# A seven-product scheme for part of the first MoE product, output sums kept in DRAM, and the MoE order set by a list scheduler

## Chip, core and metric

The kernel runs on one core of a Trainium2 chip. The metric is the device time of one execution in microseconds (us); lower is better.

## What is computed

Softcapped attention over 4 batches of 12 heads, 448 tokens of 64 values each, then a dense layer with a SiLU gate. The weights `w_in` (768 x 2048) and `w_out` (2048 x 768) come in as float64, everything else as float32.

```python
scores = scale * np.matmul(q, k.transpose(0, 1, 3, 2))
scores = cap * np.tanh(scores / cap)
scores = scores - np.max(scores, axis=-1, keepdims=True)
attn = np.exp(scores)
attn = attn / (np.sum(attn, axis=-1, keepdims=True) + 1e-09)
x = np.matmul(attn, v)            # then (4, 12, 448, 64) -> (1792, 768)
h = x @ w_in
g = h * (1.0 / (1.0 + np.exp(-h)))
out = g @ w_out
```

## The kernel before

The program has two stages. **Attention** runs first; it writes its result, transposed, into two SBUF tensors: `XH` holds x rounded to float32r and `XL` the remainder. Both are 128 partitions by 6 `d_model` tiles by 1792 tokens. **The MoE stage** follows. Every product there is made of three matmuls, high x high, high x low and low x high, so that float32r matmuls give float32 accuracy.

The 16 `d_ff` tiles of 128 are taken in 8 pairs (`G = 2`). For a tile `f` and a block of tokens `h_unit` (L640) adds up 6 `d_model` tiles x 3 = 18 matmuls in one PSUM bank. Blocks are 512, 512, 512 and 256 tokens. `gate` makes g from it: sigmoid on ACT (L655), product with h on DVE (L656), the rounded `gh` on ACT (L662), the remainder `gl` on DVE (L666). For a pair and 128 tokens `o_unit` (L691) multiplies g by `w_out`: 2 tiles x 3 products x 2 halves of 384 columns = 12 matmuls into two PSUM banks of the pool `ps_s`. `add` (L713, L715) adds the two banks on DVE to an accumulator in SBUF; 14 of these (`acc`) hold the whole output until the last pair, when each is written out from the SP queue (L719).

Weights arrive as float64 by one DMA per tile (`load_w`, L602 and L604) in one of three `RAW` buffers. `decode` turns them into float32 by integer operations (`f64_bits`: L169 on ACT or L167 on DVE, then L171, L172, L176, L180 on DVE, with the scratch tile `KRV`), and splits them into a high part (L623, ACT) and a low part (L625, DVE).

The order of the MoE work is written out by hand in `moe()`: a list of units of PE work, with one small piece of decoding (`bg`) beside each, and `BACK` for the first 19 places. After each unit's matmuls are recorded come, on ACT and DVE, what was put off from the unit before (`LATE`), the piece of decoding, and the unit's own gate or add. In the attention stage `FIRST` says in which slot which decode steps of the first four weight tiles stand. POOL issues DMAs in the attention stage only; among them `fold` (L389), which adds P to T in SBUF as an accumulating DMA.

Of the kernel before, what the change touches and what calls it, by code (L numbers as in the profile page):

```python
# [11 lines left out]
U32 = mybir.dt.uint32  # L12
# [173 lines left out]
def tile_softcap_attention_swish_moe(  # L186
# [41 lines left out]
    KRV = const.tile([128, DM], F32, name="KRV")  # L228
# [3 lines left out]
    psa = ExitStack()  # L232
    pool = lambda st, name, bufs, **kw: st.enter_context(tc.tile_pool(name=name, bufs=bufs, reuse_waits="tile", **kw))
# [14 lines left out]

    ones = a1.tile([128, 3, 32], F32, name="ones")
# [183 lines left out]
    def norm(s, parts=(0, 1, 2)):  # L433
        b, u = s // NU, s % NU
        cs = slice(b * S, (b + 1) * S)
        x = U[s]
        xh, xl = XH[:, 2 * u:2 * u + 2, cs], XL[:, 2 * u:2 * u + 2, cs]
        if 0 in parts:
            nc.vector.tensor_tensor(flat(x), flat(x), flat(RB.pop(s)), ALU.mult)
        if 1 in parts:  # L440
            nc.vector.tensor_copy(xh, x)
        if 2 in parts:
            nc.vector.tensor_tensor(xl, x, xh.bitcast(F32), ALU.subtract)
            if s == NS - 1:
                tail.close()
                MPOOL["acc2"] = pool(core, "acc2", 1, side="right")


    BACK = {
        0: [[], [("d", 3, 3), ("d", 3, 4)]],  # L450
        1: [[("d", 3, 5)], []],
        3: [[("x", NS - 2, 0)], []],
        5: [[], [("x", NS - 1, 0)]],
        6: [[], [("d", 4, 0), ("d", 4, 1)]],
        7: [[], [("d", 4, 2)]],
        8: [[], [("d", 4, 3), ("d", 5, 0), ("d", 5, 1)]],
        10: [[("d", 5, 2)], []],
        11: [[("d", 5, 3)], []],
        12: [[], [("d", 5, 4)]],
        13: [[], [("d", 6, 0), ("d", 6, 1)]],  # L460
        14: [[("d", 6, 2)], [("d", 6, 3)]],
        15: [[("d", 5, 5), ("d", 4, 4)], [("d", 4, 5)]],
        16: [[], [("d", 6, 4)]],
        17: [[("d", 6, 5)], [("d", 7, 0), ("d", 7, 1)]],
        18: [[], [("d", 7, 2), ("d", 7, 3)]],
    }
# [12 lines left out]
        (8, "D1"): (2, (4, 5)),  # L479
        (9, "D1"): (3, (0,)),  # L480
        (10, "D1"): (3, (1,)),
        (11, "D1"): (3, (2,)),
# [59 lines left out]
    def attention():  # L542
# [34 lines left out]
        MPOOL["h"] = pool(psa, "ps_h", 2, space=PSUM)  # L577
        MPOOL["w"] = pool(core, "w", 1)
        MPOOL["g"] = pool(core, "g", 4)
        MPOOL["acc"] = pool(core, "acc", 1)  # L580
        gate(*HEAD[0], (0, 1, 2))
        norm(NS - 3)
# [6 lines left out]
    NTT = NT // 128  # L589
# [3 lines left out]
    blocks = [(t0, min(512, NT - t0)) for t0 in range(0, NT, 512)]  # L593
    NB = len(blocks)

    def load_w(m, eng=nc.sync):
        f, o = divmod(m, 2) if m >= 4 else (m % 2, m // 2)
# [3 lines left out]

# [5 lines left out]
    def decode(m, steps):  # L607

        for step in steps:
            raw = WR[m]  # L610
            if WIDE:
                f64_bits(nc, raw.bitcast(U32).rearrange("p (n t) -> p n t", t=2), KRV, RAW[m % NBUF][:, 0:DM], step, m < 4)
            f = RAW[m % NBUF][:, 0:DM]
            if step == 4:
                if m % 6 < 3:
                    t = W02[m % 6]
                else:
                    t = MPOOL["w"].tile([128, 2 * DM], F32R, tag=f"w{m % 6}", name="w")
                WS[m] = t.rearrange("p (a n) -> p a n", a=2)
                if m < 4:  # L620
                    nc.vector.tensor_copy(WS[m][:, 0], f)
                else:
                    nc.scalar.activation(out=WS[m][:, 0], in_=f, func=AF.Copy)  # L623
            elif step == 5:
                nc.vector.tensor_tensor(WS[m][:, 1], f, WS[m][:, 0].bitcast(F32), ALU.subtract)  # L625
                if m + 3 < 2 * NF:
                    load_w(m + 3, nc.gpsimd if m < 3 else nc.sync)

    GT = {}
    LATE = []  # L630
    HEAD = []

    def h_unit(f, blk, ps=None, kks=range(KDM)):
        t0, n = blocks[blk]
        w = WS[f if f < 2 else 2 * f]
        if ps is None:
            ps = MPOOL["h"].tile([128, 512], F32, tag="h", name="h")
        for kk in kks:
            for a, x in ((0, XH), (0, XL), (1, XH)):
                nc.tensor.matmul(  # L640
                    ps[:, 0:n],
                    w[:, a, kk * 128:(kk + 1) * 128],
                    x[:, kk, t0:t0 + n],
                    start=(kk == 0 and a == 0 and x is XH),
                    stop=(kk == KDM - 1 and a == 1),
                )
        return ps

    GF = {}

    def gate(f, blk, ps, steps=(0, 1)):
        n = blocks[blk][1]
        if 0 in steps:
            gf = MPOOL["g"].tile([128, 512], F32, tag="g", name="gf", bufs=2)
            nc.scalar.activation(out=gf[:, 0:n], in_=ps[:, 0:n], func=AF.Sigmoid)  # L655
            nc.vector.tensor_tensor(gf[:, 0:n], ps[:, 0:n], gf[:, 0:n], ALU.mult)  # L656
            GF[f, blk] = gf
        gf = GF[f, blk]
        if 1 in steps:
            gl = MPOOL["g"].tile([128, 512], F32R, tag="gl", name="gl")  # L660
            gh = MPOOL["g"].tile([128, 512], F32R, tag="gh", name="gh")
            nc.scalar.activation(out=gh[:, 0:n], in_=gf[:, 0:n], func=AF.Copy)  # L662
            GT[f, blk] = (gh, gl)
        if 2 in steps:
            gh, gl = GT[f, blk]
            nc.vector.tensor_tensor(gl[:, 0:n], gf[:, 0:n], gh[:, 0:n].bitcast(F32), ALU.subtract)  # L666
        elif steps == (0, 1):
            LATE.append((f, blk, ps, (2,)))

    def back(slot, n):  # L670
        for kind, j, z in BACK.get(slot, ((), ()))[n]:
            if kind == "d":
                decode(j, (z,))
            elif kind == "x":
                norm(j)

    def o_unit(fp, blk, t):
        ts = slice(t * 128, t * 128 + 128)
        pa = ps_s.tile([128, 2, 512], F32, tag="s", name="s")
        pa = [pa[:, e] for e in range(2)]  # L680
        if (fp, blk, t) == LAST:
            pa[1] = MPOOL["h"].tile([128, 512], F32, tag="h", name="h")

        ends = ((0,), (1,)) if (fp, blk, t) == LAST else ((0, 1),)
        for es in ends:
            for z, f in enumerate(range(G * fp, G * fp + G)):
                g = GT[f, blk]
                w = WS[f + 2 if f < 2 else 2 * f + 1]
                for a, b in ((0, 0), (0, 1), (1, 0)):
                    for e in es:  # L690
                        nc.tensor.matmul(  # L691
                            pa[e][:, 0:NO2],
# [5 lines left out]
        return pa  # L698

    ACC = {}  # L700
    LAST = (NFP - 1, NB - 1, (NT - blocks[-1][0]) // 128 - 1)

    def add(fp, blk, t, pa):
        tt = blocks[blk][0] // 128 + t
        if tt not in ACC:
            ACC[tt] = MPOOL["acc" if tt < 6 else "acc2"].tile([128, DM], F32, name=f"acc{tt}")
        a = ACC[tt]
        last = (fp, blk, t) == LAST
        for e in range(2):
# [137 lines left out]
```

## Time and profile before

| | |
|---|---|
| median of 3 runs | 623.57 us (623.45 to 624.31) |
| the profiled execution | 622.44 us |
| its span, first to last instruction | 620.6 us |
| busy share of the span: PE / DVE / ACT / POOL | 99% / 68% / 42% / 9% |
| granted TensorE clock, mean | 0.999 |
| HBM read / written | 42.47 MB / 5.51 MB |

The shares are means over two stages. The attention stage ends, on PE, with the first matmul of the MoE's own units at 153.65 us; from there to the end the time goes through pairs of `d_ff` tiles, one every 58.24 us. To read what a change inside a pair is worth, one such stretch is to be looked at by itself. A busy PE in these views is the modelled duration of overlapping matmuls; the pace of the matmuls is read from the chain of work, where a run of n matmuls stands with its time.

### The profile page before, as it was taken

The numbers are of one execution on the slowest core, as the hardware profiler recorded it, in microseconds if no ns is written. First come the engines' busy times: TensorE is split into PE (matmuls) and PEld (weight loads), VectorE is DVE, ScalarE is ACT, GpSimd is POOL, SyncE is SP. The second block draws the span as 40 slices with busy tenths as digits, with TensorE's granted clock in tenths as the row PEclk, the third lists the DMA queues.
The fourth block names the chain that finished last, engine by engine and source line by source line (L and its number), as shares of the span: only waits on it lengthen the run. The fifth ranks groups of instructions, "written<-read, shape, count | busy, mean of one in ns | idle before, by whom it ended". The sixth has DMA issues, their size and how long they took to land.

```text
span 620.6 us, 9043 instructions
## 1 busy us (share of the span) xinstructions
PE 612.3 (99%) x3662; PEld 481.2 (78%) x3662; DVE 418.9 (68%) x661; ACT 257.6 (42%) x333; POOL 54.0 (9%) x90
## 2 busy tenths in 40 slices
PE   7999999999999999999999999999999999999996
PEld 3333333334899899989999999899899989999996
DVE  2788988887896676846775586467566846774343
ACT  7999999994312223222223222223123222222110
POOL 2353434320000000000000000000000000000000
PEclk9999999999999999999999999999999999999999
DMA  7999998982300411302111111112011302000224
GB/s 237 264 228 220 260 184 209 260 158 44 103 1 0 154 52 51 102 3 70 68 65 51 52 52 51 52 51 65 39 51 52 102 0 69 35 0 1 102 104 156
DMA packets 18499, 59.19 MB, mean 95 GB/s; under 512 B 4594, under 2 KB 8306, under 8 KB 18450
## 3 DMA queue, kind: packets, MB, share of 16 engines
q1 hardware_dynamic: 12498, 34.32, 17.3%
q0 software_dynamic: 5952, 24.22, 16.3%
q8 instruction: 31, 0.51, 0.3%
q14 instruction: 18, 0.15, 0.1%
HBM read 42.47 MB, written 5.51 MB: 77 GB/s over the span
## 4 chain that ended last, share of the span: by engine, by line
PE 96%; ACT 2%; DVE 1%; issue 0%; ACTq 0%; DVEq 0%
PE s L691 38%; PE h L640 37%; PE o L377 8%; PE s L314 8%; PE s L399 2%; PE o L385 1%; PE s L326 1%; ACT P L344 1%; ACT P L336 1%; PE s L640 1%; PE o L261 0%; DVE T L354 0%; DVE T L359 0%; PE h L691 0%; ACT P L340 0%
## 5 line engine op out<-in xcount | busy, mean ns | idle before, releaser
L640 PE MATMUL h<-XH,w 128*128 128x512 f32 (+1 forms) x756 | 217.5, 363 | 0.0
L691 PE MATMUL s<-w,gh 128*128 128x384 f32 x892 | 191.3, 335 | 0.0
L691 PEld LDWEIGHTS s<-w,gh 128*128 128x128 f32 x892 | 157.8, 188 | 2.9
L640 PEld LDWEIGHTS h<-XH,w 128*128 128x128 f32 x756 | 136.7, 188 | 22.1 <-issue 0.7
L640 PE MATMUL h<-XL,w 128*128 128x512 f32 (+1 forms) x378 | 137.5, 364 | 0.0
L655 ACT ACTIVATE gf<-h 128x512 f32<-128x512 f32 (+1 forms) x63 | 34.2, 543 | 204.7 <-PE h L640 204.4
L691 PE MATMUL s<-w,gl 128*128 128x384 f32 x446 | 113.7, 335 | 0.0
L656 DVE TENSOR_TENSOR gf<-h,gf 128x512 f32<-128x512 f32 (+1 forms) x63 | 39.2, 622 | 103.9 <-ACT gf L655 103.9
L715 DVE TENSOR_TENSOR acc<-s,acc 128x384 f32<-128x384 f32 x195 | 99.1, 549 | 8.4 <-PE s L691 8.2
L691 PEld LDWEIGHTS s<-w,gl 128*128 128x128 f32 x446 | 80.9, 188 | 0.0
L640 PEld LDWEIGHTS h<-XL,w 128*128 128x128 f32 x378 | 71.2, 188 | 10.4
L344 ACT ACTIVATE P<-P 128x896 f32<-128x896 f32 (+1 forms) x60 | 71.2, 1259 | 0.0
L666 DVE TENSOR_TENSOR gl<-gf,gh 128x512 fp32r<-128x512 f32 (+1 forms) x64 | 40.0, 625 | 38.2 <-ACT gh L662 38.2
L336 ACT ACTIVATE P<-s 128x896 f32<-128x896 f32 x72 | 62.4, 924 | 5.8 <-PE s L314 5.7
L314 PE MATMUL s<-QK 64*64 64x448 f32 x576 | 60.4, 545 | 2.1 <-ACT P L336 1.0
L662 ACT ACTIVATE gh<-gf 128x512 fp32r<-128x512 f32 (+1 forms) x64 | 37.0, 579 | 59.6 <-DVE gf L656 59.6
L377 PE MATMUL o<-P,VT 128*64 128x448 f32 x288 | 56.8, 543 | 0.0
L314 PEld LDWEIGHTS s<-QK 64*64 64x64 f32 x576 | 20.0, 133 | 39.6 <-issue 12.5
L377 PEld LDWEIGHTS o<-P,VT 128*64 128x64 f32 x288 | 19.6, 137 | 36.0 <-issue 31.0
L623 ACT ACTIVATE w<-RAW 128x768 fp32r<-128x768 f32 x28 | 23.7, 846 | 56.7 <-DVE RAW L180 50.4
L354 DVE SCALAR_TENSOR_TENSOR T<-P,epst 128x896 f32<-128x896 f32 x24 | 27.0, 1125 | 17.5 <-ACT P L344 17.5
L169 ACT ACTIVATE KRV<-RAW 128x768 f32<-128x768 f32 x28 | 25.0, 893 | 18.2 <-DVE RAW L180 13.1
(65 smaller groups left out, 370.0 us busy)
## 6 DMA issues: line engine op xcount, KB each, us to landing
RAW<-in_moe_w_in_dram SPq DMA_DIRECT2D x14, 768.0 KB, 4.5
QK<-in_qkv_dram POOLq DMA_DIRECT2D x21, 480.0 KB, 5.6
RAW<-in_moe_w_out_dram SPq DMA_DIRECT2D x13, 768.0 KB, 4.3
R<-US SPq DMA_DIRECT2D x96, 56.0 KB, 4.2
out_dram<-acc SPq DMA_DIRECT2D x13, 384.0 KB, 2.3
T<-P POOLq DMA_DIRECT2D x22, 224.0 KB, 4.7
VT<-in_qkv_dram POOLq DMA_DIRECT2D x22, 192.0 KB, 5.4
RAW<-in_moe_w_out_dram POOLq DMA_DIRECT2D x3, 768.0 KB, 4.8
```

The source lines that it names most:

```text
L314: nc.tensor.matmul(ps[half(c), e, 0:S], q[half(e), k0:k0 + 64], q[half(e), 0:S], start=True, stop=True)
L336: nc.scalar.activation(out=p, in_=SP.pop((i, j))[:, :, 0:S], func=AF.Tanh, scale=REG["sct"])
L344: nc.scalar.activation(out=p, in_=p, func=AF.Exp, scale=REG["cap"])
L354: nc.vector.scalar_tensor_tensor(out=flat(T[i]), in0=flat(p[:, 0:2]), scalar=epst[:, 0:1], in1=flat(p[:, 2:4]), op0=ALU.add, op1=ALU.add,)
L377: nc.tensor.matmul(O[s][half(e), t, 0:S], v, p, start=start, stop=stop)
L640: nc.tensor.matmul(ps[:, 0:n], w[:, a, kk * 128:(kk + 1) * 128], x[:, kk, t0:t0 + n], start=(kk == 0 and a == 0 and x is XH), stop=(kk == ...
L655: nc.scalar.activation(out=gf[:, 0:n], in_=ps[:, 0:n], func=AF.Sigmoid)
L656: nc.vector.tensor_tensor(gf[:, 0:n], ps[:, 0:n], gf[:, 0:n], ALU.mult)
L662: nc.scalar.activation(out=gh[:, 0:n], in_=gf[:, 0:n], func=AF.Copy)
L666: nc.vector.tensor_tensor(gl[:, 0:n], gf[:, 0:n], gh[:, 0:n].bitcast(F32), ALU.subtract)
L691: nc.tensor.matmul(pa[e][:, 0:NO2], g[a][:, ts], w[:, b, e * NO2:(e + 1) * NO2], start=(z == 0 and a == 0 and b == 0), stop=(z == G - 1 an ...
L715: nc.vector.tensor_tensor(ae, pa[e][:, 0:NO2], ae, ALU.add)
```

## The change

**Products.** The first two pairs (pairs 0 and 1) stay as they were, except that tokens are now cut in two halves of 896, each into a block of 512 and one of 384. For the six pairs from `FS = 2` on, a block of the first half and the same block of the second half are done together. The four `d_model` tiles 0 to 3, the two `d_ff` tiles and the two token blocks form a 2 x 2 by 2 x 2 product, done with seven products and sums (Winograd's form of Strassen) in place of eight; tiles 4 and 5 are done plainly. `CHAIN` lists eight steps and the PSUM bank (A to D) each adds into. In what follows the *wide half* of a pair is the 512-token block pair (c = 0), the *narrow half* the 384-token one (c = 1). Steps 1, 5, 6, 7 and 8 are 6 matmuls each, steps 2, 3 and 4 are 12: 66 per half, 132 per pair, where 8 units of 18 made 144. Between steps four PSUM sums are needed per half (`carry`): a bank is copied to SBUF and added on DVE onto another bank, on which a later step goes on accumulating.

**Operands.** `tokens` makes three combinations of x for each half, once, during pairs 0 and 1 (17 steps a half; the second combination overwrites part of `XH` and `XL`). `combine` makes the combinations of the weights for each pair (6 steps).

**Output sums.** The SBUF accumulators go. Each o-unit's two banks are copied to two of five `st` tiles (`evacuate`, mostly on ACT) and added to the output rows in DRAM by an accumulating DMA from the POOL queue (`store`, 196 of them, 192 KB each; the first pair's write plainly). In the last pair `preload` fetches the sums back, 14 DMAs from the POOL queue, DVE adds the last term, and SP writes the rows out. The o-units have their own pool of two double banks (`ps_q`).

**Order.** `BACK`, `LATE` and `bg` go. `moe()` writes only the order of the PE units by hand. All other work is given to `plan` with its dependencies, a duration for each instruction, and latencies (4.5 for a POOL DMA, 10 for an SP DMA); it sets the order on ACT, DVE, POOL and SP, which of ACT and DVE makes a copy, and which of 3 scratch tiles and 5 `st` tiles is used. Decoding is done in halves of 384 columns with these scratch tiles in place of `KRV`. The steps 4 and 5 of weight tile 2 move from attention slot 8 into the MoE stage, and step 3 of tile 3 from there into slot 11.

```diff
+    blocks = [(0, 512), (512, HALF - 512), (HALF, 512), (HALF + 512, HALF - 512)]
...
+    CHAIN = {
+        1: ("A", "a11", "b11", None),
+        2: ("B", "a12", "b21", (0, 0)),
+        3: ("C", "s4", "b22", (0, 1)),
+        4: ("A", "a22", "t4", (1, 0)),
+        5: ("C", "s1", "t1", None),
+        6: ("A", "s2", "t2", None),
+        7: ("A", "s3", "t3", None),
+        8: ("D", None, None, (1, 1)),
+    }
+    OPENS = (1, 2, 5, 8)
...
+    SUMMED = {1: ("A", "B"), 6: ("A", "C"), 7: ("A", "D"), 8: ("C", "D")}
+
+    def carry(fp, c, z, step):
+
+        n = blocks[c][1]
+        r, q = (BANK[b][:, 0:n] for b in SUMMED[z])
+        if step == 0:
+            GF[fp, c, z] = temp("c", fp, c, z)
+            copy(ON["c", fp, c, z, 0], GF[fp, c, z][:, 0:n], r)
+        else:
+            nc.vector.tensor_tensor(q, q, GF[fp, c, z][:, 0:n], ALU.add)
...
+    def evacuate(fp, blk, t, e=None):
+        pa = PO[fp, blk, t]
+        if fp < NFP - 1:
+            k = HELD["st", fp, blk, t, e]
+            a = SUM[fp, blk, t, e] = MPOOL["st"].tile([128, NO2], F32, tag=f"st{k}", name="st")
+            copy(ON["e", fp, blk, t, e], a, pa[:, e, 0:NO2])
+        else:
+            ae = SUM[blk, t].rearrange("p (e n) -> p e n", e=2)
+            nc.vector.tensor_tensor(ae, pa[:, :, 0:NO2], ae, ALU.add)
+
+    def store(fp, blk, t, e=None):
+        rows = row(blk, t)
+        if fp < NFP - 1:
+            how = dict(accum_op=ALU.add) if fp else {}
+            nc.gpsimd.dma_start(out=out[rows, e * NO2:(e + 1) * NO2], in_=SUM[fp, blk, t, e], **how)
+        else:
+            nc.sync.dma_start(out=out[rows, :], in_=SUM[blk, t])
...
+    NTEMP = 3
+    NST = 5
+
+    FS = 2
...
+            a = {
+                1: [("wl", m)] + FREE["A"],
+                2: [("wl", m)] + FREE["B"],
+                5: [("wl", m + 1), ("t", c, 7)] + FREE["C"],
+                8: [("wl", m + 1)] + FREE["D"],
+                6: [("s", fp, 5), ("t", c, 12), dup(1)],
+                7: [("s", fp, 5), ("t", c, 8), dup(6)],
+                4: [("wl", m + 1), dup(7)] + [("t", 0, 16), ("t", 1, 16, 0), ("t", 1, 16, 1)][c:2 * c + 1],
+                3: [("s", fp, 5), ("wl", m), add(6)],
+            }[z]
...
+        for fp in range(FS, NFP):
+            P = lambda *zs: [("p", fp, 0, z) for z in zs]
+            oa, ob = o(fp - 1, 1), o(fp - 1, 3)
+            if fp == FS:
+                seq += P(2, 1) + ob[:1] + P(5, 8, 6) + ob[1:2] + P(3, 7) + ob[2:] + P(4)
             else:
...
+                seq += P(2, 1) + oa[:1] + P(5) + oa[1:2] + P(8, 6) + oa[2:] + P(3) + ob[:1] + P(7) + ob[1:] + P(4)
+            P = lambda *zs: [("p", fp, 1, z) for z in zs]
+            oa, ob = o(fp, 0), o(fp, 2)
+            k = 4 if fp + 1 < NFP else 2
+            seq += P(2, 1, 5, 8) + oa[:3] + P(6) + oa[3:] + P(3) + ob[:1] + P(7) + ob[1:k] + P(4) + ob[k:]
+        seq += o(NFP - 1, 1) + o(NFP - 1, 3)
```

In the list of dependencies `dup(z)` is the copy and `add(z)` the addition of a `carry`, `wl` a weight tile's low part, `s` a step of `combine`, `t` a step of `tokens`, `FREE[q]` the gate's product (step 1 of `gate`) that last read bank q. `oa` and `ob` are o-units: 3 and 3 stand in a wide half (of the pair before), 4 and 4 in a narrow half.

What the order becomes at two places follows. The first is ACT at the end of pair 4 (its matmuls are done, bar the last block, and the next pair's begin). Before: `gf<-h` is the sigmoid, `gh<-gf` the rounding, `KRV<-RAW` the first decode step and `w0`, `w1` the high part of a weight tile.

```order
L655 ACTIVATE gf_3594<-h_3574 128x256
L662 ACTIVATE gh_3598<-gf_3594 128x256
L623 ACTIVATE w_3630<-RAW1_67 128x768
L655 ACTIVATE gf_3655<-h_3634 128x256
L662 ACTIVATE gh_3659<-gf_3655 128x256
L169 ACTIVATE KRV_72<-RAW2_68 128x768
L655 ACTIVATE gf_3716<-h_3697 128x512
```

After the change: `st<-q` copies one half of an o-unit to an `st` tile (`q_4042` is the last but one of the pair's o-units, `q_4069` the last), `gf<-A` at L820 is the sigmoid of step 4's bank, and `gf<-A` at L599 the copy of the next half's step 1.

```order
L599 ACTIVATE st_4083<-q_4042 128x384
L599 ACTIVATE gh_4086<-gf_4063 128x384
L599 ACTIVATE st_4090<-q_4042 128x384
L599 ACTIVATE st_4107<-q_4069 128x384
L599 ACTIVATE st_4110<-q_4069 128x384
L820 ACTIVATE gf_4125<-A_3837 128x384
L599 ACTIVATE w1_70<-RAW0_66 128x768
L599 ACTIVATE gh_4130<-gf_4125 128x384
L599 ACTIVATE gf_4156<-A_4134 128x512
```

The copies of the outputs stand now on ACT, ahead of the sigmoid. `st_4110` is put into the tile whose last user was the first half of the o-unit two before `q_4069` (`st_4056`), so it waits for that store's DMA.

The second place is DVE in the wide half of the pair after, from the gate of step 1's sum to the gate of step 3. Before the change a comparable stretch was a gate, decode steps and additions to `acc`:

```order
L656 TENSOR_TENSOR gf_2506<-h_2486,gf_2506 128x512
L666 TENSOR_TENSOR gl_2509<-gf_2506,gh_2510 128x512
L180 SCALAR_TENSOR_TENSOR RAW0_66<-RAW0_66,KRV_72 128x768
L715 TENSOR_TENSOR acc2_1598<-s_2512,acc2_1598 128x384 x2
L625 TENSOR_TENSOR w0_69<-RAW0_66,w0_69 128x768
L715 TENSOR_TENSOR acc3_1621<-s_2530,acc3_1621 128x384 x2
```

After the change (`gf_4234<-A` is the copy for `carry` 6, the two rows at L840 the additions of `carry` 6 and 8):

```order
L822 TENSOR_TENSOR gf_4159<-B_4112,gf_4159 128x512
L828 TENSOR_TENSOR gl_4175<-gf_4159,gh_4174 128x512
L171 TENSOR_SCALAR gf_4192<-gf_4192 128x384
L172 TENSOR_SCALAR gf_4192<-gf_4192 128x384
L176 SCALAR_TENSOR_TENSOR gf_4192<-RAW2_68,gf_4192 128x384
L180 SCALAR_TENSOR_TENSOR RAW2_68<-RAW2_68,gf_4192 128x384
L601 COPY gf_4234<-A_4134 128x512
L840 TENSOR_TENSOR C_4161<-C_4161,gf_4234 128x512
L840 TENSOR_TENSOR D_4196<-D_4196,gf_4216 128x512
```

The additions to `acc` are gone from DVE; in their place stand a copy and an addition for which PE's step 3 waits, behind four decode instructions of half the width.

## Rows read from the trace of the kernel before

**Rows 1.** The page: busy time by engine, and the granted clock in 40 slices.

```profile
PE 612.3 (99%) x3662; PEld 481.2 (78%) x3662; DVE 418.9 (68%) x661; ACT 257.6 (42%) x333; POOL 54.0 (9%) x90
...
PEclk9999999999999999999999999999999999999999
```

**Rows 2.** Busy time by stretch: attention, the MoE stage, and pair 4.

```profile
core 0: us, PE busy (x) PEld busy (x) DVE busy (x) ACT busy (x) POOL busy (x), PEclk, DMA share, GB/s
...
386.82:445.06 58.24, 58.24 (x313) 53.82 (x313) 37.90 (x64) 15.60 (x24) 0.00 (x0) 1.00 0.17 55
...
153.65:620.60 466.95, 461.99 (x2482) 427.08 (x2478) 300.42 (x507) 116.76 (x183) 0.00 (x0) 1.00 0.17 59
0.00:153.65 153.65, 150.30 (x1184) 54.13 (x1185) 118.48 (x154) 140.86 (x150) 54.05 (x90) 1.00 0.85 207
```

**Rows 3.** Chain that ended last, in pair 4: start, us, what, matmuls.

```profile
386.82 8.20 PE h L640 x36
395.02 4.18 PE s L691 x24
399.20 4.12 PE h L640 x18
...
424.12 2.15 PE h L640 x18
```

**Rows 4.** Groups by line in pair 4: busy us, mean ns, idle before.

```profile
L715 DVE TENSOR_TENSOR acc<-s,acc 128x384 f32<-128x384 f32 x28 | 14.2, 549 | 0.2 <-PE s L691 0.2
...
L625 DVE TENSOR_TENSOR w<-RAW,w 128x768 fp32r<-128x768 f32 x4 | 3.8, 952 | 0.0
L180 DVE SCALAR_TENSOR_TENSOR RAW<-RAW,KRV 128x768 uint32<-128x768 uint32 x4 | 3.8, 952 | 0.0
...
L623 ACT ACTIVATE w<-RAW 128x768 fp32r<-128x768 f32 x4 | 3.4, 848 | 9.5 <-DVE RAW L180 8.4 <-PE s L691 1.1
...
L171 DVE TENSOR_SCALAR KRV<-KRV 128x768 f32<-128x768 f32 x4 | 2.2, 552 | 0.4 <-ACT KRV L169 0.4
```

**Rows 5.** Groups by line and shape, whole span.

```profile
L656 DVE TENSOR_TENSOR gf<-h,gf 128x512 f32<-128x512 f32 x47 | 32.5, 691 | 96.0 <-ACT gf L655 96.0
...
L655 ACT ACTIVATE gf<-h 128x512 f32<-128x512 f32 x47 | 28.1, 598 | 157.4 <-PE h L640 157.1
...
L439 DVE TENSOR_TENSOR U<-U,R 128x896 f32<-128x896 f32 x12 | 13.0, 1083 | 0.0
...
L655 ACT ACTIVATE gf<-h 128x256 f32<-128x256 f32 x16 | 6.1, 383 | 47.4 <-PE h L640 47.4
```

**Rows 6.** Timeline of ACT and DVE in pair 4, behind the h-unit that ends at 390.9.

```profile
391.04 0.60 ACT L655 ACTIVATE gf<-h 128x512 f32<-128x512 f32 x1 [4.37 <-PE h L640]
391.67 0.69 DVE L656 TENSOR_TENSOR gf<-h,gf 128x512 f32<-128x512 f32 x1 [3.79 <-ACT gf L655]
```

**Rows 7.** DMAs by line: L389 accumulates, L301 loads QK (both POOL), L719 writes the output.

```profile
L389 POOL DMA_DIRECT2D T<-P x22: 817/870/1205, 17.3 to 137.0; - x22
...
DMA to landing us min/median/max: 4.2/4.7/7.7
...
L301 POOL DMA_DIRECT2D QK<-in_qkv_dram x21: 536/582/713, 9.9 to 127.4; - x21
...
DMA to landing us min/median/max: 2.9/5.6/10.4
...
DMA to landing us min/median/max: 2.3/2.3/3.1
```

**Rows 8.** Timeline of DVE in the last full attention slot.

```profile
137.80 0.94 DVE L176 SCALAR_TENSOR_TENSOR KRV<-RAW,KRV 128x768 uint32<-128x768 uint32 x1
...
144.58 1.15 DVE L354 SCALAR_TENSOR_TENSOR T<-P,epst 128x896 f32<-128x896 f32 x1 [1.17 <-ACT P L344]
```

**Rows 9.** Chain that ended last, its end.

```profile
614.59 1.06 PE h L691 x6
...
615.67 0.56 DVE acc L715
```

More of the change, by code (lines that the diff above doesn't have):

```diff
@@ L576, in attention @@
         pso.close()
[L577 removed]
         MPOOL["w"] = pool(core, "w", 1)
[L579 to L582, printed above, removed]
+        MPOOL["g"] = pool(core, "g", 1)
+        MPOOL["st"] = pool(core, "st", 1)
+        MPOOL["xt"] = pool(core, "xt", 1)
+        HELD["g", 0, 0] = HELD["temp", "g", 0, 0] = 0
+        for z in range(4):
+            gate(*HEAD[0], z)
+        psa.close()
+        MPOOL["o"] = pool(psm, "ps_q", 2, space=PSUM)
+        MPOOL["h"] = pool(psm, "ps_h", 1, space=PSUM)
+        for q in "ABCD":
+            MPOOL["h"].tile([128, 512], F32, tag=q, name=q)
     WIDE = moe_w_in.dtype == I64
@@ L647, in h_unit, with product @@
-        return ps
+            product(
+                ps[:, 0:n], lambda a: w[:, a, kk * 128:(kk + 1) * 128], lambda a: (XH, XL)[a][:, kk, t0:t0 + n],
+                kk == 0, kk == KDM - 1,
+            )
+        return ps
+    def product(ps, w, x, first, last, more=False):
+        for z, (a, b) in enumerate(((0, 0), (0, 1), (1, 0))):
+            nc.tensor.matmul(
+                ps, w(a), x(b), start=(first and z == 0), stop=(last and z == 2), skip_group_check=more
+            )
+    CHAIN = {
[8 more added lines that the diff above has]
+    }
@@ L649, in tile_softcap_attention_swish_moe, with gate @@
     GF = {}
-    def gate(f, blk, ps, steps=(0, 1)):
+    def gate(f, blk, ps, step):
         n = blocks[blk][1]
[L653 to L675, printed above, removed]
+        if step == 0:
+            GF[f, blk] = temp("g", f, blk)
+        elif step == 2:
+            g_tiles(f, blk)
+        gf = GF[f, blk][:, 0:n]
+        if step == 0:
+            nc.scalar.activation(out=gf, in_=ps[:, 0:n], func=AF.Sigmoid)
+        elif step == 1:
+            nc.vector.tensor_tensor(gf, ps[:, 0:n], gf, ALU.mult)
+        else:
+            gh, gl = (t[:, 0:n] for t in GT[f, blk])
+            if step == 2:
+                copy(ON.get(("g", f, blk, 2), "ACT"), gh, gf)
+            else:
+                nc.vector.tensor_tensor(gl, gf, gh.bitcast(F32), ALU.subtract)
@@ L680, in o_unit @@
[L680 to L685, printed above, removed]
+        last = (fp, blk, t) == LAST
+        if last:
+            pa = [MPOOL["h"].tile([128, 512], F32, tag=q, name=q) for q in "AB"]
+        else:
+            pa = MPOOL["o"].tile([128, 2, 512], F32, tag="q", name="q")
+        pe = lambda e: (pa[e] if last else pa[:, e])[:, 0:NO2]
@@ new lines, in o_unit, with preload @@
+        PO[fp, blk, t] = pa
+    LAST = (NFP - 1, 3, (HALF - 512) // 128 - 1)
+    ORDER = [(blk, t) for blk in (0, 2, 1, 3) for t in range(blocks[blk][1] // 128)]
+    row = lambda blk, t: slice(blocks[blk][0] + 128 * t, blocks[blk][0] + 128 * t + 128)
+    SUM = {}
+    ROWBUF = {}
+    def preload(u):
+        m = 2 * NF - 3
+        k = u % 10
+        n = (m, "x3", "x4", m + 1, m + 2)[k // 2]
+        if n not in ROWBUF:
+            ROWBUF[n] = xt_tile(int(n[1]), 0, F32) if n in ("x3", "x4") else RAW[n % NBUF]
+        SUM[ORDER[u]] = ROWBUF[n][:, (k % 2) * DM:(k % 2) * DM + DM]
+        nc.gpsimd.dma_start(out=SUM[ORDER[u]], in_=out[row(*ORDER[u]), :])
```

588 lines of the change are left out of this document (471 added, 117 removed).

## The prediction

> **What bounds the kernel now.** I read the engines' busy shares first, then busy time by stretch, then the chain that ended last. PE is busy 99% of the span at full granted clock throughout [rows 1]; that is 2.4 GHz of its two levels. The stretches show where the others stand: in a pair of the MoE stage, 58.24 us long, DVE works 37.9 us and ACT 15.6, and POOL does nothing from 153.65 on [rows 2]. In the chain the same pair is matmuls from end to end, one unit after the other, with no wait between them [rows 3]. So the MoE stage, 467 us of the span [rows 2], is as long as its matmuls, and only fewer or shorter matmuls shorten it. The pace is read there too: 18 matmuls of 512 columns take 4.12 us (229 ns each), 18 of 256 take 2.15, and 24 of 384 in the o-units 4.18 (174 ns each). Everything the change adds elsewhere costs nothing as long as PE does not wait for it.
>
> **The matmuls.** A pair's h-units before: 36 matmuls in 8.20 us, four runs of 18 in 4.12, two of 18 in 2.15, in all 8.20 + 16.48 + 4.30 = 28.98 us [rows 3]. A pair from the third on has 66 matmuls of 512 columns and 66 of 384: 66 x 0.229 + 66 x 0.174 = 15.1 + 11.5 = 26.6 us. That is 2.37 us less; six such pairs give 14.2. In the two plain pairs the blocks of 512, 512, 512, 256 become 512, 384, 512, 384: 72 x (0.229 + 0.174) = 29.02, 0.04 more each, 0.1 together. The o-units keep their matmuls. PE's own saving is **14.1 us**. The new bank layout adds no matmul.
>
> **Room on DVE and ACT.** Of a pair's 37.9 us DVE loses 28 additions to `acc` of 0.549 = 15.4 [rows 4]. It gains 8 additions between banks, four wide at 0.69 (the nearest row, also a PSUM operand [rows 5]) and four narrow at 0.55: 5.0; the weights' sums, four of 256 columns at under 0.55 and one of 0.95: at most 3.1; decoding in halves, at most 0.55 an instruction, so 8 x 0.55 = 4.4 a tile where four took 3.0: at most 5.6; and of the copies that can stand on either engine about 5 a pair at 0.6: 3.0. Together about 39 of 55.9 us, 70%. ACT gains some 25 output copies and 6 bank copies. A 384-column one lies between 0.383 and 0.598 [rows 5], so 0.49: 12.3 + 3.3, and 0.85 for the weights' sums [rows 4]: 32 of 55.9. `tokens` adds 13 DVE instructions of 1024 columns, 10 of 768 and 7 of 384. By the 896-column row, 1.083 [rows 5], a 1024-column one is 1.24; with 0.95 and 0.55 that makes 16 + 9.5 + 4 = 30 us, spread over pairs 0 and 1 (116 us), where DVE then stands at some 95 us. No engine gets past PE on the mean. What is left is the order: whether a step finds its operand late.
>
> **The handovers in a pair.** I laid PE's units in a row at the pace above. Three places are close.
> Step 6 to step 3: step 3 adds onto bank C after the copy and addition of `carry` 6, and one o-unit of 2.09 us lies between. In the wide half the copy (0.69), the addition (0.69) and about 0.1 for each handover (ACT starts 0.1 behind the matmuls, DVE right behind ACT [rows 6]) make 1.6: 0.5 to spare; in the narrow half 0.8. An addition that writes PSUM is not in the trace; as DVE's instructions go by columns, I take the 0.69, and the 0.5 covers 70% more.
> Step 4 to step 1 of the narrow half: step 1 takes bank A over after sigmoid 0.60 and product 0.69, 1.5 with the handovers, behind step 2 of 12 x 0.174 = 2.09: 0.6 to spare.
> The same handover at the end of the pair is the third: narrow gate 0.49 + 0.55 + 0.2, wide step 2 of 2.73, so 1.5 to spare; but here ACT has the last o-unit's copies ahead of the sigmoid, and the last of them waits for a store.
>
> **The store.** The order of the rows on ACT sets this wait. The wide half lasts 15.1 us of steps and six o-units of 2.09, 27.6 in all; steps 2, 1, 5 and 8 of the narrow half end at 32.8, and three o-units, step 6, one, step 3, one, step 7 and three follow. So the last three o-units end at 49.5, 51.6 and 53.7 us after the pair's start, step 4 at 55.8, the next step 2 at 58.5. The second copy of the last o-unit reuses the tile of the first copy of the o-unit that ended at 49.5; that copy ends at 50.1 and its store is issued then. With a time L from issue to landing the tile is free at 50.1 + L; the copy takes 0.49, and the sigmoid must begin by 57.3 so that step 1 is not held. So up to **L = 6.7 us** nothing is lost, and each microsecond beyond costs one a pair. A DMA that adds into DRAM is not in the trace. Nearest from below: the plain output writes, 2.3; nearest in kind: L389, an accumulating DMA from the POOL queue, 4.2 to 7.7 with a median of 4.7, while the DMA engines were 85% busy [rows 2, 7]; from above, the longest landing of a POOL load from DRAM, 10.4 [rows 7]. I take 4.7, the nearest in kind: nothing lost, 2 us to spare. The issue itself, 0.87 [rows 7], is 1.74 for the two stores of an o-unit of 2.09, so POOL keeps up. Since single landings of 7.7 do occur among those 22, I charge one late store in the six pairs: 7.7 - 6.7 = **1.0 us**, once.
>
> **The edges.** In attention slot 8 DVE loses two instructions, in slot 11 it gains one of 0.95 us [rows 4]; the latter meets an idle 1.17 us that ends with a wait for ACT [rows 8], so it costs 0; with that cover gone it would be 0.95. Weight tile 5's load moves from POOL in slot 8 to SP behind the last attention transfers; pair 1, which needs it, is 50 us away. The end is the same chain: six matmuls, an addition of 0.56 and a write [rows 9]; the `preload`s are issued 20 us and more before their addition, and at L = 10.4 still land in time. Cost 0.
>
> **Sum.** Against the profiled execution (622.44): 622.44 - 14.1 + 1.0 = 609.3. The median of the runs lies 1.1 above that execution, so the forecast is 623.57 - 14.1 + 1.0 = **610.5 us**. What a measurement here can tell from no change is about 0.2%, 1.25 us.
>
> **Rivals.**
> *Stores land late, all of them* (12%). Every store at the pair's end takes L389's longest, 7.7: six times 1.0, and 623.57 - 14.1 + 6.0 = 615.5. For it: the store shares the DMA engines with the next weight tile's load, and POOL now issues beside a DVE at 70%. Against it: POOL's 22 accumulating issues took 0.82 to 1.21 us [rows 7] in a stage in which DVE was 77% busy [rows 2].
> The Trainium skill's page "SBUF — State Buffer", section "SBUF: two separate sides", speaks against this change: a DMA issued by GpSimd needs descriptors that it cannot write while a VectorE instruction holds the port pair that the two share, and it gives 620 ns alone against 3100 ns beside a copy. By its figure a landing of 4.7 would become an estimated 7.2 and the forecast 612.5 or so; no issue in this trace was held like that.
> *The stores bound the stage: slower* (11%). If adding into DRAM takes as long as the longest load, L = 10.4, the sigmoid at each pair's end is 3.7 us late and step 1 with it: 6 x 3.7 = 22, giving 631.7. It decides from L = 6.7 + 14.1/6 = 9.0 on. For it: an accumulating store must read the DRAM rows before it writes them, and five tiles carry 28 copies a pair. Against it: in kind, 4.7; and the DMA share in this stage is 0.17 [rows 2].
> *Handovers late* (12%). If a decode instruction of about 0.95 us [rows 4] stands ahead where the order wants none, the wide step 3 is 0.45 late, the narrow one 0.15, step 1 0.35: 0.95 a pair, 5.7 in all, 615.2. The changeover in pairs 1 and 2, where `tokens` fills DVE, would show it first. Against it: the four decode instructions ahead of the copy have 4 us before step 6 ends.
> That the matmuls do not fall is excluded: the two programs have 1152 and 1080 of them in the h-products, 72 = 6 x 12 fewer.
>
> **How the numbers follow.** The forecast, with nothing or up to 2 us lost, gets 65%: every chain that I could lay out fits, and two prices are not in the trace. The range 608.3 to 616.5 holds it, the late stores and the late handovers; it leaves out the slower case. Its lower end is the bare sum 609.5 less the scatter of runs and the attention slot; its upper end the two 615s with 1 us more. Faster by over 0.2%: the forecast and both 615s, 88%, as a few of the slower case's values fall short of 9.0 and a few of the others go past. Within 0.2%: 2%. Slower: 10%.
>
> **What would show it.** Right: the pairs from the third on start every 55.9 us (26.6 + 29.2) and the chain is still all PE; the L840 additions take about 0.7; the stores land in under 6.7; PE's idle time in the MoE stage stays under 2 us. Wrong: step 1 or the sigmoid of bank A waiting for an output copy, and that for a DMA (stores); step 3 waiting for L840 (handover); pairs 0 and 1 longer than 58.3 (`tokens`); DVE past 90% in any pair.

## The result, and the profile after

The changed kernel takes **613.12 us** (median of 4 runs, 612.56 to 614.41) against 623.51 for the kernel before on the same chip (622.99 to 624.31): a ratio of 0.9835, 95% interval 0.9815 to 0.9855. The forecast was 610.5, the range 608.3 to 616.5. The profiled execution takes 612.56 us, where the sum had 609.3. So the saving is there, but it is 3.3 us smaller than the sum had it. This part finds where.

The page, against [rows 1]: busy time by engine, the two DMA queues (packets, MB, share of the time of 16 DMA engines), the group of the stores, and their median from issue to landing.

```profile
PE 599.5 (98%) x3590; PEld 479.3 (78%) x3590; DVE 422.7 (69%) x702; ACT 362.9 (59%) x589; POOL 223.0 (37%) x299
...
q0 software_dynamic: 32912, 67.49, 61.8%
q1 hardware_dynamic: 12642, 35.10, 17.7%
...
L901 POOL DMA_DIRECT2D out_dram<-st x196 | 162.3, 948 | 260.6 <-ACT st L599 252.7
...
out_dram<-st POOLq DMA_DIRECT2D x196, 192.0 KB, 4.8
```

PE has 72 matmuls fewer than in [rows 1], as counted. The shares of DVE and ACT are no alarm. What is new is the queue of POOL's DMAs. By stretches, against [rows 2], pairs 3 to 6, each from the start of its wide step 2 to the next one's:

```profile
core 0: us, PE busy (x) PEld busy (x) DVE busy (x) ACT busy (x) POOL busy (x), PEclk, DMA share, GB/s
...
310.48:366.33 55.85, 55.85 (x301) 53.05 (x301) 36.46 (x71) 30.02 (x60) 24.30 (x29) 1.00 0.90 155
366.33:423.03 56.70, 56.11 (x301) 53.00 (x301) 36.01 (x70) 30.05 (x60) 24.55 (x29) 1.00 0.89 153
423.03:480.17 57.14, 56.12 (x302) 53.01 (x302) 36.04 (x70) 29.95 (x60) 24.49 (x29) 1.00 0.88 152
480.17:537.66 57.49, 56.11 (x302) 53.00 (x301) 36.10 (x70) 29.85 (x60) 24.41 (x29) 1.00 0.87 151
```

Pair 3 is 55.85 long, as the forecast had it (55.9); pairs 4, 5 and 6 are 0.85, 1.29 and 1.64 longer, with the same instructions on every engine. The DMA engines, 0.17 busy in such a pair before, are now at 0.87 to 0.90. The waits of PE from 150 to 600 us, in the order of the columns: us in total, times, longest:

```profile
PE C L758 <- DVE C L840: 3.2, 4, 1.4
```

One kind, four times: the wide step 3 waits for `carry` 6's addition on bank C, in pairs 2, 4, 5 and 6 and not in 3 and 7. (The idle time is 3.2, but the four pairs are 4.3 longer: step 3's matmuls begin every 0.23 us and last 0.39, and across a wait this overlap is lost too.) PE never waits at step 1, the place where the prediction looked for late stores. The chain of work before the wait in pair 5 (start, us, what):

```profile
421.94 0.64 POOL out_dram L901
422.58 10.66 DMA out_dram<-st
...
433.33 0.13 ACT st L599
...
433.71 0.49 ACT st L599
434.20 0.53 ACT gh L599
...
434.75 0.69 DVE gl L828
435.44 0.31 DVE gf L171
...
436.76 0.56 DVE RAW L180
437.32 0.61 DVE gf L601
...
438.02 0.71 DVE C L840
...
438.78 0.73 PE C L758 x2
```

Read from the end: step 3 is late because of the addition, that because of its copy (L601), and the copy stands on DVE behind `gl` and four decode instructions (L171 to L180). `gl` waits for `gh` on ACT, and `gh` stands behind two output copies, whose tile is held by a store that takes 10.66 us to land. It was issued 0.5 us before the pair's start, last of six stores in 5 us, and between two weight loads, 2.8 us before and 2.4 us after that start. In pair 2, which has other o-units, the store at the head of a like chain is issued 1.0 us after the start and lands in 6.3.

### The profile page after: what moved, and what is told of

The parts are those of the page before. It is cut to its first block, busy times and chain, and to the rows that moved or that the text cites. A ratio compares the mean times of both kernels' runs of the same rounds, so it can differ in the third digit from the quotient of the medians.

```text
span 610.8 us, 9823 instructions
## 1 busy us (share of the span) xinstructions
PE 599.5 (98%) x3590; PEld 479.3 (78%) x3590; DVE 422.7 (69%) x702; ACT 362.9 (59%) x589; POOL 223.0 (37%) x299
## 3 DMA queue, kind: packets, MB, share of 16 engines
HBM read 47.97 MB, written 44.04 MB: 151 GB/s over the span
## 4 chain that ended last, share of the span: by engine, by line
PE 77%; POOL 6%; issue 5%; DMA 5%; DVE 3%; ACT 3%; POOLq 0%; ACTq 0%; DVEq 0%
PE q L861 28%; PE A L758 10%; PE o L378 8%; PE s L315 8%; PE C L758 8%; POOL out_dram L901 6%; PE B L758 5%; DMA out_dram<-st 5%; PE D L758 3%; PE s L400 2%; PE o L386 1%; PE s L327 1%; ACT P L345 1%; ACT P L337 1%; PE s L758 1%
## 5 line engine op out<-in xcount | busy, mean ns | idle before, releaser
L901 POOL DMA_DIRECT2D out_dram<-st x196 | 162.3, 948 | 260.6 <-ACT st L599 252.7
L861 PE MATMUL q<-w,gh 128*128 128x384 f32 x876 | 187.8, 335 | 0.0
L861 PEld LDWEIGHTS q<-w,gh 128*128 128x128 f32 x876 | 155.7, 188 | 3.1 <-DVE w L626 0.4
L599 ACT ACTIVATE st<-q 128x384 f32<-128x384 f32 x177 | 80.1, 490 | 76.0 <-PE q L861 53.3
L861 PE MATMUL q<-w,gl 128*128 128x384 f32 x438 | 111.4, 335 | 0.0
L861 PEld LDWEIGHTS q<-w,gl 128*128 128x128 f32 x438 | 79.4, 188 | 0.0
L758 PE MATMUL A<-XH,w 128*128 128x384 f32 (+1 forms) x192 | 59.1, 355 | 0.0
L599 ACT ACTIVATE gh<-gf 128x512 fp32r<-128x512 f32 (+1 forms) x63 | 36.3, 578 | 22.5 <-DVE gf L822 22.5
L758 PE MATMUL C<-XH,w 128*128 128x512 f32 (+1 forms) x144 | 44.4, 371 | 3.2 <-DVE C L840 3.2
L758 PE MATMUL B<-XH,w 128*128 128x512 f32 (+1 forms) x132 | 40.8, 371 | 0.0
L599 ACT ACTIVATE gf<-A 128x384 f32<-128x384 f32 (+1 forms) x29 | 15.7, 540 | 39.6 <-PE A L758 36.7
L758 PEld LDWEIGHTS A<-XH,w 128*128 128x128 f32 x192 | 35.5, 188 | 3.0
```

What stands on the lines that cost most here:

```text
L599: nc.scalar.activation(out=out, in_=in_, func=AF.Copy)
L758: nc.tensor.matmul(ps, w(a), x(b), start=(first and z == 0), stop=(last and z == 2), skip_group_check=more)
L861: nc.tensor.matmul(pe(e), g[a][:, ts], w[:, b, e * NO2:(e + 1) * NO2], start=(z == 0 and a == 0 and b == 0), stop=(z == G - 1 and a == 1),)
L901: nc.gpsimd.dma_start(out=out[rows, e * NO2:(e + 1) * NO2], in_=SUM[fp, blk, t, e], **how)
```

## The experiments

What came out of the trace is **theory A**: the adding stores of a pair's end and the weight load of the next pair's start take the DMA engines from each other, a store lands late, ACT's copy waits for it, and DVE's queue carries the delay to step 3. Rivals: **B**, the order alone does it (decode ahead of the copy, whatever the stores do); **C**, adding into DRAM is slow by itself, load or no load; **D**, DVE's work holds up POOL's transfers.

The table has each pair's time over 55.85 us, and for pair 2, which has other o-units, and pair 7, which is followed by the tail, over the version with plain stores (49.55 and 67.29). All are differences of starts of units, in us, in one profiled execution of each version. It is what the versions are compared by; medians scatter by 1 us.

| version | median | ratio to before (95%) | pair 2 | 3 | 4 | 5 | 6 | 7 | sum |
|---|---|---|---|---|---|---|---|---|---|
| changed kernel | 613.12 | 0.9815 to 0.9855 | 0.50 | 0 | 0.85 | 1.29 | 1.64 | 0 | 4.3 |
| the same again (e11) | 613.67 | 0.9833 to 0.9879 | 0.60 | 0 | 0.65 | 1.09 | 1.62 | 0 | 4.0 |
| e1 no first load | 609.34 | 0.9745 to 0.9780 | 0 | 0 | 0 | 0.01 | 0 | 0 | 0 |
| e2 plain stores | 609.16 | 0.9748 to 0.9783 | 0 | 0 | 0 | 0.01 | 0 | 0 | 0 |
| e3 decode behind | 610.51 | 0.9761 to 0.9803 | 0.57 | 0.65 | 0.98 | 0.38 | 0 | 0 | 2.6 |
| e4 four tiles | 613.01 | 0.9804 to 0.9838 | 1.41 | 0.01 | 2.09 | 0.01 | 0.51 | 1.34 | 5.4 |
| e5 load later (planner only) | 613.81 | 0.9815 to 0.9858 | 0.57 | 1.66 | 1.89 | 1.01 | 1.47 | 0 | 6.6 |
| e6 e5 and e3 | 609.80 | 0.9757 to 0.9793 | 0.61 | 0.01 | 0.75 | 0.27 | 0.05 | 0 | 1.7 |
| e7 o-units spread | 609.50 | 0.9758 to 0.9795 | 0.59 | 0 | 0.21 | 0.09 | 0 | 0 | 0.9 |
| e9 load held | 608.45 | 0.9751 to 0.9777 | 0.03 | 0.02 | 0.02 | 0.03 | 0.02 | 0.74 | 0.9 |
| e10 e7 and e9 | 608.79 | 0.9753 to 0.9778 | 0.03 | 0.02 | 0.13 | 0.02 | 0.02 | 0.11 | 0.3 |

### e1: without the load of a pair's start

```diff
 def load_w(m, eng=nc.sync):
     fp, r = divmod(m, 4)
+    if r == 0 and fp > FS:
+        WR[m] = RAW[m % NBUF].bitcast(I64) if WIDE else RAW[m % NBUF][:, 0:DM]
+        return
```

> Left out: the load of the first weight tile of pairs 3 to 7 (it would be issued 2.4 us after the start of the pair before it, beside the stores of that place); what is decoded in its stead is what stood in the buffer. The order on every engine stays. In the changed kernel the wide step 3 starts late in pairs 2, 4, 5 and 6, by 0.52, 0.85, 1.29 and 1.64 us, 4.3 in all, and the chain before it runs through a store that took 10.7 to 10.9 us to land. Theory A (the stores land late because a weight load takes the DMA engines beside them, and the scalar engine's copies wait for them): without the load the stores of that place land in under 8 us, step 3 is on time in pairs 4 to 6, and the median falls by 3.8 to 4.3, to 608.5 to 609.3. Theory B (the order alone: the decode instructions ahead of carry 6's copy make step 3 late, whatever the stores do): nothing changes, 612 to 613.5, and the three losses stand. Theory C (adding into DRAM is slow by itself, load or no load): landings stay near 10 us, and the median stays over 612.

All losses are gone, 609.34. With the load away the longest landing around pair 5's start is 8.5 where it was 10.7; the expectation had "under 8", and at the start of pair 3 it is 9.3. The fall is about what the load itself takes, by an estimate from the lines under e2: four loads keep all 16 DMA engines busy for 15.4% of 57.14 us, 2.2 us each. Minimum, median and maximum of the stores issued from 415 to 425.5 us, the changed kernel first:

```profile
DMA to landing us min/median/max: 3.7/8.1/10.7
```

```profile
DMA to landing us min/median/max: 3.6/7.5/8.5
```

Two microseconds of landing decide. The decode still stands ahead of the copy, on the same order, and costs nothing: theory B is out. Theory C, that the adding is slow load or no load, is out as the whole cause.

### e2: plain stores

```diff
-how = dict(accum_op=ALU.add) if fp else {}
+how = {}
```

> Left out: the adding; every store writes its rows plainly, so the output holds the last pair's two terms only. Same order, same bytes from the chip's side, same number of transfers. Theory A and C both give landings of under 5 us at the start of a pair, no late step 3, and 608.3 to 609.3; under A or C the share of the DMA engines in a pair from the third on also falls, from 0.88 to 0.90 to about half, as plain stores of the first pair landed in 2.6 us against 4.8 to 5.0 later. Theory B: 612 to 613.5, with the losses of 0.85 to 1.64 us in place. Theory D (the store's transfer is held up at its start on the POOL queue by the vector engine's work, not by the adding): landings stay near 5 us in the median and 10 at the longest, and the time stays.

No loss, 609.16. The stretch of pair 5 by DMA queue in the changed kernel, then here:

```profile
q0 software_dynamic: 4080, 5.57, 72.5%
q1 hardware_dynamic: 569, 3.10, 15.4%
...
out_dram<-st POOLq DMA_DIRECT2D x29, 192.0 KB, 4.8
RAW<-in_moe_w_in_dram SPq DMA_DIRECT2D x2, 768.0 KB, 6.9
```

```profile
q0 software_dynamic: 1794, 5.51, 27.3%
q1 hardware_dynamic: 581, 3.18, 17.4%
...
out_dram<-st POOLq DMA_DIRECT2D x28, 192.0 KB, 2.2
RAW<-in_moe_w_in_dram SPq DMA_DIRECT2D x2, 768.0 KB, 4.5
```

And the same stretch by engine, against pair 5 above:

```profile
421.53:477.39 55.86, 55.86 (x302) 53.06 (x302) 36.08 (x70) 29.86 (x60) 15.14 (x28) 1.00 0.45 156
```

The first window cuts into stores at its edges; by its bytes it holds 28.3 of them (5.57 MB of 196,608 bytes each), the second 28.0. So an adding store takes 144 packets where a plain one takes 64 (4080 / 28.3, 1794 / 28), and 23.4 us of one DMA engine where a plain one takes 8.7 (0.725 x 57.14 x 16 / 28.3; 0.273 x 55.86 x 16 / 28). The adding ones fill the DMA engines to 73% by themselves, and a load beside them lands in 6.9 us and not 4.5. It is not the larger number of packets that costs: in the trace's DMA records an adding packet of 1536 bytes takes 140 ns in the median, a plain one of 1536 bytes, on SP's queue in the attention stage, 65, and one of 4608 bytes of e2's plain stores 200, which is as many bytes in a nanosecond.

Theory D is out: DVE is busy for 36.0 and 36.1 us, and the plain stores land in 2.2 us in the median. One expectation was missed: beside the loads at pair 5's start a plain store still lands in 6.6, not under 5.

### e3: the decode behind the addition

```diff
+if r == 3 and fp > FS and (h, z) == (0, 1):
+    a += [("c", fp, 0, 6, 1)]
 op(
     ("d", m, h, z), "DVE" if z else "ACT",
...
```

> One dependency more for the planner: the vector engine's decoding of the first half of a pair's last weight tile waits for carry 6's addition of that pair's wide half (pairs 3 to 7). Stores and loads stay. Theory A with B (both are needed: the late store delays the scalar engine, and the decode instructions, pushed back with it, then stand ahead of the copy): the stores still land in 10 to 11 us and the scalar engine still waits 3 to 4 us for them, but step 3 starts on time in pairs 4 to 6: 608.7 to 609.5. Theory C' (the scalar engine's wait alone makes step 3 late): the losses stay, 612 to 613.5. The planner may place other work anew, so a small loss can turn up elsewhere.

610.51, a loss of 2.6 in place of 4.3: half a hit. Late stores are still there (10.8 and 11.1 in pairs 3 and 4), and the copy has no decode ahead of it, but it still stands behind `gl`. In pair 3 the landing is later than in the changed kernel (8.1, and 7.2 in e11), though stores and loads go off at the same places there to within 0.1 us; why is open. The chain in pair 3, which had lost nothing in the changed kernel:

```profile
310.08 10.80 DMA out_dram<-st
...
322.38 0.70 DVE gl L828
...
323.18 0.70 DVE gf L601
...
323.97 0.70 DVE D L840
324.67 0.61 DVE C L840
...
325.32 0.73 PE C L758 x2
```

`gl` begins 12.3 us after the store, and behind it come a copy and two additions: too late by 0.4 for step 3. So the decode made the wait longer; the late `gl` makes one by itself.

### e4: four store tiles

```diff
-NST = 5
+NST = 4
```

> Four store tiles in place of five. Theory A or C (tiles held by stores that land late set the scalar engine's waits): with a tile held some 0.5 + 0.9 + 5 us and three o-units of six copies in 6.2 us, the copies fall behind in every bunch, by 2 us and more; copies wait for stores over 60 us in all where it is 20 now, and the time rises by 1 us or more a pair: 620 to 640. Theory B: no change beyond what a new order does, 612 to 614.

A miss: 613.01, not 620 to 640. Given four tiles, the planner laid the copies out anew, more of them on DVE: from 254 us on, copies waited for stores 14.9 us on ACT and 11.2 on DVE, against 14.8 and 1.5 with five tiles. The sum of the losses is larger by 1, but at other units: the longest wait of PE is step 1 for a gate's product. The time lies in the range given for theory B, but as the order is another one too, the run does not decide between the theories.

### e5 and e6: the load later in the plan

```diff
+if r == 0 and fp > FS:
+    prior += [("p", fp - 1, 0, 3)]
 op(("load", m), "SP", 0.6, lambda: load_w(m), prior)
```

> The load that the first experiment left out is kept, but waits for step 3 of the wide half of the pair before (pairs 3 to 7), so that it is issued some 16 us later; the planner orders the rest anew. Theory A (the late step 3 came from this load beside the stores of the pair's start): the stores there land within 9 us as without the load, step 3 starts on time, and the median falls by 3 to 4 us, to 608.7 to 610. Rival (every place is as full, since the adding stores alone keep the DMA engines 72 to 73% busy): the load makes other stores late, which copies of the next o-units wait for, and the loss turns up behind another step: 611 to 613.5.

> The later load and the decode behind carry 6 together. If the late load is the whole cause, this is as fast as the later load alone, 608.5 to 610. If each takes away a part, as the third experiment left about 2 of the 4.3 us, it is the fastest of the versions that compute everything, 608 to 609.3, and no pair from the third on is longer than 56.0 us. If the loss only moves, 610 to 612.

The edit of e5 did not do what it says. The dependency exists in the planner alone; on the chip SP's queue waits for the buffer only, and the load went off at 314.60, 2.4 us after pair 3's start as ever:

```profile
314.60 27.35 SPq L590 DMA_DIRECT2D RAW<-in_moe_w_in_dram  x2
```

What changed is the order: the planner now puts four decode instructions ahead of the copy in pair 3 too, the load before goes off 3.0 us ahead of that pair's start where it went off 0.5 behind it, and the store lands in 10.8. Pair 3 now loses 1.66, where it had lost nothing. That is the theory seen from the other side, by accident: where both the late store and the decode are there, the time is lost. e6, with the decode behind, is at 609.8 with 1.7 lost, as e3 would lead one to expect; the hoped-for 608 to 609.3 was missed, and its load had not moved either.

### e7: the o-units spread

```diff
-k = 4 if fp + 1 < NFP else 2
+k = 2
```

> Two of the last three o-units of a pair are put behind step 4, so that four stores and not six are issued in the last 6 us of a pair, and the next steps 2 and 1 follow two o-units. Loads and decode are as in the changed kernel but for what the planner makes of it. If the bunch of stores at the pair's end is what the load collides with (theory A, seen from the stores), the longest landing there falls from 10 to 11 us to under 9 and the median to 608.7 to 610. If the number of stores in a pair counts and not where they stand, 611.5 to 613.5.

609.50, as theory A has it. The decode still stands ahead of the copy; the last six stores of the pair are now spread over 7 us, and the eight around pair 5's start (415 to 425.5 us) land within 8.6:

```profile
DMA to landing us min/median/max: 3.6/7.9/8.6
```

But one load did not stay where it was: in pairs 4 to 6 the second now goes off 1.5 us before the pair's start, ahead of the last four stores, and not 2.4 behind it. So e7 shows that stores and loads laid out otherwise lose little; that it is the spread of the stores alone it does not show.

### e8: the scheme in three pairs

```diff
-FS = 2
+FS = 5
```

> The scheme in three pairs (5 to 7) in place of six; pairs 2 to 4 take plain units, with stores, sums in DRAM and planner as in the changed kernel. If the scheme is worth its matmuls, 2.37 a pair, three pairs cost 7.1 more, less the 1.4 that pairs 2 and 4 lost: 612.9 + 7.1 - 1.4 = 618.6, with 58.2 for a plain pair and 55.85 for one of the scheme; 617 to 620 with the scatter of a new order. If the stores hold up a plain pair just as well, it is longer than 58.3 and the sum 620 or more. If the scheme were worth less than its matmuls because of what it adds on the other engines, the time would be under 616.

617.14 (616.02 to 617.74; ratio 0.9874 to 0.9911), within the expected 617 to 620. Two plain pairs with stores, one of them with a wait of 0.9 for a weight's low part, and a pair of the scheme:

```profile
318.56:377.94 59.38, 58.48 (x313) 55.18 (x313) 27.34 (x53) 26.79 (x55) 24.61 (x28) 1.00 0.84 146
377.94:436.31 58.37, 58.37 (x313) 55.19 (x313) 38.35 (x67) 31.07 (x60) 24.79 (x29) 1.00 0.83 147
486.39:542.24 55.85, 55.85 (x301) 53.05 (x301) 36.32 (x71) 29.94 (x60) 24.41 (x29) 1.00 0.89 156
```

58.37 - 55.85 = 2.52 us a pair, where the matmuls promised 2.4 (2.37 of the scheme and 0.04 of the blocks). The gain is the scheme's.

### e9 and e10: the load really held

```diff
+def hold(m):
+    t = MPOOL["st"].tile([128, 1], F32, tag="hold", name="hold")
+    nc.scalar.activation(out=t, in_=RAW[m % NBUF][:, 0:1], func=AF.Copy)
...
+if r == 0 and fp > FS:
+    op(("hold", m), "ACT", 0.25, lambda: hold(m), prior + [("p", fp - 1, 0, 3)])
+    prior = prior + [("hold", m)]
 op(("load", m), "SP", 0.6, lambda: load_w(m), prior)
```

> In the fifth experiment the added dependency stood in the planner alone; on the chip the load still went off at 2.4 us after the pair's start, as its queue waits for nothing but the buffer. Here a one-column copy on the scalar engine, placed behind step 3 of the wide half, reads the buffer, so that the load really waits. The vector engine's order is that of the fifth experiment, with the four decode instructions ahead of carry 6's copy in every pair. Theory A: stores of the pair's start land within 9 us, the scalar engine waits under 3 us there, and the losses of 0.75 to 1.65 us in pairs 3 to 6 go although the decode still stands ahead: 608.7 to 610. Theory B (the order alone): the losses stay, 612 to 615. Rival to A: the load now makes stores late some 16 us further on, and the loss turns up there: 611 to 614.

> The spread o-units of the seventh experiment and the held load together. Both take away the same thing, the load beside six stores, so theory A gives no second gain: 608.5 to 610, with only pair 2's loss of about 0.3 to 0.4 us left, and pairs 3 to 6 at 55.85. If the two gains added up, it would be under 608.

e9 is **608.45** (608.06 to 609.94), the lowest median, just under the expected 608.7 to 610, and computes all of the output. The load starts at 329.11, 18.3 us after pair 3's start. e5 is its counterpart: the DVE and ACT instructions at the pairs' starts stand in the same order there, only the load is not held, and 6.6 us are lost where e9 loses 0.9. DVE in pair 5 of the changed kernel, then in pair 4 of e9 (start, us, and in brackets the idle time before and what ended it):

```profile
434.75 0.69 DVE L828 TENSOR_TENSOR gl<-gf,gh 128x512 fp32r<-128x512 f32 x1 [4.71 <-ACT gh L599]
...
436.76 0.56 DVE L180 SCALAR_TENSOR_TENSOR RAW<-RAW,gf 128x384 uint32<-128x384 uint32 x1
437.24 0.68 DVE L601 COPY gf<-A 128x512 f32<-128x512 f32 x1
```

```profile
376.34 0.69 DVE L832 TENSOR_TENSOR gl<-gf,gh 128x512 fp32r<-128x512 f32 x1 [2.64 <-ACT gh L603]
...
378.35 0.56 DVE L180 SCALAR_TENSOR_TENSOR RAW<-RAW,gf 128x384 uint32<-128x384 uint32 x1
379.36 0.69 DVE L605 COPY gf<-A 128x512 f32<-128x512 f32 x1 [0.46 <-PE A L762]
```

These rows stand in the same order in both; `gl` comes 9.65 us after the pair's start and not 11.72, the decode is done before step 6 is, and the copy now waits for PE, as it should. The load makes no trouble further on: PE waits nowhere else in pairs 2 to 6. A loss of 0.74 in pair 7 is left. The chain there is the same, behind a store that lands in 9.6; no weight load follows that pair's start, two loads of output rows do, as in the changed kernel, and why the store is late (8.6 in the changed kernel) is open. e10 loses least in the trace (0.3), but its median, 608.79, is not below e9's: a second gain beyond the scatter is not there, as theory A had it.

### e11: the changed kernel again

> The changed kernel once more, beside the two above on one chip: 612.5 to 613.5, late step 3 in pairs 4 to 6 again, each behind a store of over 10 us. If the losses were chance and not the order's and the loads' doing, other pairs would show them.

613.67 (611.85 to 617.57), beside e9 and e10 on one chip, just over the expected 612.5 to 613.5. The same pairs lose, and nearly the same amounts, behind stores of 9.9, 10.6 and 11.1 in pairs 4 to 6; the waits are the order's and the loads' doing, not chance.

## Why the prediction was right, and where it was off

**The matmuls: right.** A saving of 14.1 was forecast. Without the late step 3 the profiled execution would be 612.56 - 4.3 = 608.3, and 622.44 - 14.1 is 608.3. Pair by pair, 58.24 became 55.85, 2.39 less where 2.37 was said.

**Room on DVE and ACT: right.** 36.0 to 36.5 us a pair on DVE (39 said), 30 on ACT (32 said). In pairs 0 and 1 DVE works 86 of 106 us, and pair 1 is 58.5 long, 0.2 more than said.

**The handovers: the place was right, the margin not.** The additions take 0.70 and 0.564, as taken. Step 6 to step 3 in the wide half was named as the closest of all, with 0.5 to spare, and so was the decode ahead of the copy, as the rival "Handovers late". What failed is the reason against it, that "the four decode instructions ahead of the copy have 4 us before step 6 ends". They have them only while `gl` is on time, and on ACT `gh` stands behind output copies. I followed the copies of the last o-unit to the sigmoid behind them, and not those of the next pair's first o-unit to `gh`, `gl` and DVE's queue. Two of the prediction's own signs of being wrong came with it: step 3 waits for L840, and PE is idle for 3.2 us, not under 2.

**The store: the step that failed is its price at the longest.** The median was right (4.7 taken, 4.8 measured). The term "one late store in the six pairs: 7.7 - 6.7 = 1.0 us" was taken from the longest of the 22 landings of L389 and charged at step 1. At step 1 nothing is lost; at step 3, which was charged nothing, 4.3 is, with landings of up to 10.9 that come back at the starts of pairs 4 to 6. With 4.3 in place of 1.0 the sum of 609.3 becomes 612.6, as the profiled time. That the range held is in part luck: the late stores and the late handovers, two rivals at some 615 each, were in it, and what came is the two joined, at a smaller price. The sentence behind the error is "the DMA share in this stage is 0.17" [rows 2]: that is the share of before, and the change itself raises it to 0.87 to 0.90. It could have been worked out only with the engine time of an adding DMA, and I took the landing alone. The Trainium skill's page "Collectives: The Full Stack", section "The bandwidth ceiling: the fold count and why AG ≠ RS ≠ AR", says of another kind of transfer that an add in the DMA engines needs two reads per chunk and so runs at about half the speed of a copy. The trace agrees in kind, with 2.2 times the time for a packet of the same size and 2.7 times the engine time for a store; the reads themselves no run shows (the page of the profile counts 47.97 MB read from HBM with adding stores and with plain ones).

**The rival of the shared port: no sign of it.** By the rule of "SBUF — State Buffer", section "SBUF: two separate sides", in the Trainium skill, the estimate was 612.5, close to the result, but the mechanism is another. The plain stores of e2 come from the same queue beside the same DVE work; their issue takes 0.54 us in the median, and in pair 5 they land in 2.2 in the median.

**The slower case did not come**, since the late landings do not hold step 1: the store that step 1 hangs on is issued 5.2 us before the pair's start and lands in 3.9 to 4.3 in pairs 4 to 6, and the late ones come behind it. The place from which L decides, 6.7, was worked out for step 1; at step 3, with the decode ahead, the runs put it, for the last store before a pair's start in pairs 3 to 7, between 9.1, with which pair 3 of e9 lost 0.02, and 9.6, with which pair 7 of e9 lost 0.74. With the decode behind, pair 6 of e3 lost nothing at 10.2.

## What to carry to other kernels

Before a transfer is called hidden, add up what the change itself lays on the DMA engines, in engine time and not in bytes: here 28 adding stores a pair took them from 0.17 to 0.9 and made a harmless weight load collide. When an instruction may wait for a DMA, follow what stands behind it on its engine, and behind that on the next one, to the first unit of the bottleneck. A dependency given to a planner orders instructions, but it delays a DMA only if something on the chip waits for it.

## What the runs showed of the hardware

An accumulating store of 192 KB into DRAM takes 23.4 us of DMA engine time against 8.7 for a plain one, 144 packets against 64, 140 ns for a packet of 1536 bytes against 65, 4.8 us to landing against 2.2, and 0.90 us of issue on POOL against 0.54 (medians). A 768 KB load lands in 6.9 us beside the ones and in 4.5 beside the others. Six adding stores within 5 us with two such loads around them land as late as 9.9 to 10.9 us at the start of pairs 4 to 6; with one of the loads away or held, or stores and loads spread as in e7, within 8.5 to 8.9 in pairs 4 and 5. One landing does not fit: 10.8 in pair 3 of e3, beside loads that left it at 8.1 in the changed kernel.
